# A fused attention and feed-forward kernel: small products in one 64x64 form, states by 48-wide updates

## The chip, the cores and the metric

The kernel runs on one core of a Trainium2 chip. A core has TensorE (PE in the profile; its weight loads are PEld), VectorE (DVE), ScalarE (ACT), GpSimd (POOL), SyncE (SP, which issues the loads and stores here) and 16 DMA engines. TensorE reads SBUF and writes PSUM, eight banks of 2 KB for each of 128 partitions. The metric is device time in microseconds of one launch.

## The reference

Inputs are fp32 or float64; batch 4, 8 heads, 768 tokens, head size 48, model width 384.

```python
for t in range(S):                                   # attention, per batch and head
    cur = np.einsum('bhd,bhe->bhde', u[None] * kt, vt)
    y[:, :, t] = np.einsum('bhd,bhde->bhe', rt, state + cur)
    state = wt[:, :, :, None] * state + np.einsum('bhd,bhe->bhde', kt, vt)
...
h = gelu(x @ w_in)                                   # x = y, heads side by side
u, v = h[..., :512], h[..., 512:]
v_n = (v - mean(v)) / sqrt(var(v) + 1e-6) * g_ln
v_s = einsum('ts,bsd->btd', w_sg, v_n) + b_sg        # over the 768 tokens
x = x + (u * v_s) @ w_out
...
gate = sigmoid(causal convolution of x over 5 tokens)
out = (gate * (x @ w_val)) @ w_out2
```

## The kernel before

**Attention** is worked in chunks of C = 64 tokens. A unit is one batch, one segment of 256 tokens (four chunks, NC) and one pair of heads (head 0 on partitions 0 to 63, of which 48 hold data, head 1 on 64 to 127); `unit(n)` holds its steps and there are 48 of them, 12 to a batch. The words in the order list are the steps' letters with a number. F and E: scans along the tokens for the decay factors (`suffix`, `prefix`). L and K: r and k times these factors. t and s: `turn`, two 128x128 transposes of k, and `scores`, eight 64x64 products of k and r into one PSUM bank, which m masks. B: `kv`, k by v for each chunk, and in batches 0 and 1 (`SUMMED = 2`) two products of r*k (q) with `u_col` for the r*u*k sums. o (`own_v`): the sums times v into y. d, a, S, p and D: `kv_out` copies kv's product into a strided tile, `states` runs a scan of 288 elements over it, `s_part` and `keep` copy the states out, `chunk_decay` spreads the decays. C: `tokens`, for each chunk the states and the masked scores by v. y: `y_out` adds to y on VectorE.

Both heads share a product in `kv` and `tokens`: the contraction runs over 128 rows, the right side is 96 wide and holds zeros where a head does not belong (tiles SE, `sv` and `vcd`; `pack_v` writes the zeros of `sv` on the host, `v_rows`, word v, copies into `vcd`). These are 128x64 forms: 128 rows, 64 columns of the array. In batches 2 and 3 `bonus` makes the r*u*k sums from loads of r and k by token (rk): a product on GpSimd, one on VectorE with `u_bc`, a VectorE reduction, a GpSimd product with v.

**The rest** works on half batches of 384 tokens. Each fp32 operand is split into two fp32r parts, and three 128x128 matmuls make one product (`PASS`). `xT` transposes y; `hv` makes v (512 wide) and layer norm in `ln`; `u_step` makes u; `vs_step` multiplies v_n by w_sg and scales (vso); `gated` forms u times that (gate); `wo_step`, `conv`, `val_step` and `out_step` follow. Accumulators of xT, hv, u, vs and val come from the PSUM pool psD (tag d, three buffers), those of wo and out from psC (c0 to c2), those of attention from psA (a0 and a1, one bank each) and in batch 0 also from psC and psD.

Weights arrive as float64 bits and are turned into fp32 by five passes on ScalarE and VectorE (`to_f32`, word dec) and split (`split`, spl: a copy on ScalarE, a remainder on GpSimd). In batch 0 `warm` puts three and two bf16 matmuls of 256 columns ahead of each `kv` and `tokens`; 16 of 512 columns (wps) stand at the start.

Batch b+1's attention is interleaved with batch b's rest; batch 0's attention stands alone at the start, beside the weights. All calls are recorded under words (`u13`, `vs7`, `C20`; at most `SIZE` calls to a word) and then issued in the order of `SCHEDULE`, a list written out in the source of some 2,600 words. Each engine works its own calls in that order; SP's loads have their places in the same list (pk, sv, rk, nat, wl, sg).

Of the kernel before, what the change touches and what calls it, by code (L numbers as in the profile page):

```python
# [15 lines left out]
F32 = mybir.dt.float32  # L16
# [7 lines left out]
DM = H * D  # L24
# [20 lines left out]
SV = 2 * NC * D  # L45
# [6 lines left out]
SIZE = dict.fromkeys(("hv", "u", "vs", "wo", "val", "out", "ln"), 3)  # L52
SIZE.update(dict.fromkeys("FvS", 2), z=2)

SCHEDULE = """
pk0 z0 zp4 pk1 ld0 ld1 nat0 pk2 zp0 pk3 wl0 wps0 zp7 zp5 zp1 zp3 a0 zp8 zp11 zp2 F0 wl2 D0 K0 E0 wl1
nat1 zp9 pk4 zp6 F1 L0 sv3 q0 K1 a3 E1 sv0 t0 t1 F2 k0 L1 pk5 v0 s0 a1 q1 K2 B0 v1 m0 E2 sg2 zp12 D1
zp13 k1 F3 L2 t2 o0 d0 s1 k2 sv1 a0 o0 B1 E3 D2 dec0 sv6 q2 L3 s2 o1 m1 v3 dec0 sg1 K3 d1 m2 dec1
dec0 o1 t3 wl3 dec2 dec1 pk6 v2 B2 a1 pk7 dec0 dec1 pk8 q3 o2 F4 d2 sv2 o2 D3 k3 sg0 a2 dec2 K4 s3
E4 B3 zp10 S1 F5 L4 S0 dec2 C1 K5 m3 v4 a2 t4 sv13 wl4 pk9 d3 sv7 k4 dec1 dec2 sv9 q4 B4 E5 sv5 dec0  # L60
t5 pk11 s4 k5 dec2 sv8 D4 C0 p0 a3 o4 pk10 d4 o4 spl0 y1 dec1 o3 S2 C2 o3 F6 p2 spl0 D5 nat2 S3 y0
sv4 C3 a4 v5 sv10 L5 spl1 y2 D6 E6 spl4 p1 spl2 q5 L6 y3 xT0 spl5 F7 s5 K6 S4 B5 m4 xTo0 E7 spl1 v6
m5 xTo0 xT1 F8 t6 hv0 K7 k6 d5 hv0 xTo1 q6 dec3 K8 xTo1 B6 a5 E8 D7 hv1 spl3 q7 L8 o6 d6 F9 s6 spl2
hv1 m6 q8 t7 t8 hv1 L7 k8 a6 dec4 hv0 o5 dec4 ln0 dec3 D8 dec4 k7 E9 p3 s7 ln1 F10 L9 S5 q9 v8 B8
spl3 ln0 S6 sg3 dec3 wl5 ln0 p6 v7 dec3 B7 o6 dec3 o5 ln0 C6 spl9 K9 m7 o7 d7 p4 a7 ln0 s8 spl9 p5
C5 ln1 dec4 o7 t9 E10 k9 d8 K10 nat3 pk12 v10 dec4 D9 spl5 v9 B9 y5 wl8 ld2 wl6 a8 spl4 F11 s9 d9
v11 C4 ln0 sg4 sg5 pk13 y6 S7 C7 y4 a9 K11 D10 dec5 m8 q12 t10 ln1 m9 E11 t11 k11 ln1 o8 S8 dec5 o8
q10 L10 p7 o9 y7 xT2 k10 F12 spl7 B10 o9 spl10 q13 D11 L11 dec5 xT3 s10 xTo3 K12 E12 S9 q11 B11 L12
d10 m10 xTo2 dec5 spl10 pk14 wl7 sv11 xTo2 hv2 xTo3 hv2 dec5 spl7 s12 F13 spl11 wl9 s11 ln1 spl11
t12 dec6 hv2 m11 dec6 C8 ln1 dec7 m12 d11 E13 hv3 k12 spl6 hv3 o10 v12 dec7 C9 a10 K13 S10 q14 t13  # L70
dec7 hv3 D12 dec6 spl8 dec7 o11 dec6 ln2 o11 y9 C10 a11 L13 ln2 S11 C11 spl8 ln3 dec6 o10 B12 a13
y11 dec7 ln2 nat4 sv12 pk15 y10 spl13 F14 D13 spl13 d12 o12 v13 y8 a12 ln2 xT4 xT5 spl12 E14 s13 ln2
spl12 a12 dec9 xTo4 L14 xTo4 hv4 S12 K14 ln2 ln3 hv4 xTo5 pk16 dec8 hv4 k13 dec8 spl6 xTo5 hv5 F15
u0 o12 u0 dec9 ln3 hv5 dec8 ln3 C12 dec9 dec8 B13 dec9 dec8 u0 dec9 spl14 wl12 hv5 E15 o13 wl10 D14
sv14 wl13 spl14 wl11 ln3 m13 a14 F16 ln5 s14 ln4 L15 vs0 y12 u1 q15 ln3 ln4 t14 vs0*2 a15 K15 ln4
dec10 u1 uo0 dec10 pk17 dec10 spl15 dec10 vs1 ln4 d13 dec10 K16 ln4 u1 a13 vs1 k14 ln4 cw0 ln5 D15
vs1 uo1 vs0 E16 ln5 dec12 vs1 dec11 m14 vs2 dec12 S13 vs2 ln5 dec11 vs0 ln5 dec12 dec11 s15 F17 ln5
vs2 dec12 vs2 ix1 dec13 C13 v14 dec13 vs0 o13 dec11 vs2*2 i0 dec13 dec11 B14 dec12 dec13 spl17 vs1
d14 dec13 spl17 spl16 vs1 vso2 wl15 sv15 wl14 wl16 t15 vso0 vs3 k15 spl16 gate0 vs3 m15 vs3 gate0
spl15 vso1 o14 vs3 a14 vs3 ix2 dec15 t16 gate0 vs3 v15 dec15 u2 o14 S14 y13 u2 dec15 L16 u2 gate1  # L80
dec14 dec15 p14 s16 p12 spl18 dec14 E17 C14 p13 spl18 gate1 B15 gate1 dec14 dec16 K17 u3 o15 dec14
d15 o15 uo2 wo0 dec16 D16 wo1 q16 wo4 dec14 q17 u3 spl19 dec16 u3 dec15 spl19 vso3 wo2 uo3 m16 wo5
k16 gate2 L17 sg6 sv16 u5 y14 gate2 dec16 wo3 pk19 pk18 u4 gate3 u5 a15 gate3 u5 spl20 dec16 S15 t17
gate3 spl20 s17 gate2 v16 C15 ix0 spl21 sg7 B16 sv17 wo8 spl21 d16 y15 uo5 q18 u4 spl22 u4 sg8 k17
F18 spl22 spl23 wo6 D17 wo9 E18 v17 xT6 spl23 sg9 wo7 uo4 woo0 xTo6 wo10 F19 spl24 vs4 woo0 sg10
spl24 vs4 x20 woo0 o16 wo11 woo1 cv0 L18 vs4 sg11 nat5 woo2 woo1 B17 a16 spl25 woo2 spl25 woo1 spl26
u6 m17 S16 cv0 u6 spl26 xTo6 u6 spl27 cv0 x22 vs4 spl27 v18 vs4 cv0 vs4 woo2 o16 x21 K18 xT7 cv1
# [12 lines left out]
x23 t24 woo4 ln7 hv9 x24 a23 cv3 hv8 woo4 o23 k24 o23 y22 S23 wo23 cv3 hv8 K26 cv4 bon0 v24 C23 cv4  # L100
woo5 hv8 y23 x25 cv4 woo5 hv9 m24 D25 bon0 ln8 hv9 F27 val3 ln9 bon0 val3 ln7 ln8 rk1 sv24 xT10 ln7
B24 xTo10 cv4 s25 v25 xTo10 t25 ln8 cv3 d24 hv10 L26 woo5 hv10 bon0 cv4 cv5 hv10 m25 cv4 a24 val3
ln10 E27 val4 k25 cv5 S24 xT11 valo3 B25 xTo11 C24 cv3 valo3 cv5 D26 s26 sv26 L27 outo1 nat7 valo3
val4 bon1 xTo11 t26 cv3 val4 ln8 cv3 u8 bon1 val5 valo4 val5 bon1 valo4 val5 cv5 ln8 rk2 pk28 u8
valo4 ln8 out9 cv5 hv11 a25 ln10 cv5 bon1 k26 out11 ln9 hv11 ln10 bon2 out10 valo5 u8 y24 ln9 F28
out12 uo8 hv11 ln9 u9 ln10 ln9 K27 u9 bon2 ln11 pk29 ln9 out14 d25 ln10 vs8 valo5 u9 ln10 valo5 vs8
uo9 ln11 out15 u10 m26 vs8 ln11 bon2 vs8 ln11 rk3 sv25 E28 u10 ln11 a25 s27 ln11 u10 S25 out13 v26
ix6 vs8*2 bon2 B26 vso8 C25 gate8 u11 K28 L28 gate8 D27 u11 gate8 uo10 ix7 t27 d26 vs9 outo3 k27
bon3 vs9 outo3 vs10*2 bon3 i2 u11 bon3 y25 vs9 rk4 pk30 a26*2 out16 F29 vs10 D28 outo4 out17 m27
wo24 outo5 vs10 S26 wo25 bon4 v27 vs9*2 bon4 vs9 K29 B27 vso9 C26 v28 a27 bon4 gate9 s28 rk5 sv27  # L110
nat8 p25 sv28 d27 vs10 p24 a27 p26 uo11 vs10 gate9 vs11 vso10 vs11 E29 vs11 gate10 L29 vs11 gate9
# [12 lines left out]
pk36 uo15 K35 vs15 S33 m34 E35 vs14 wo36 y32 L35 xTo14 vs15 bon8 ix10 pk37 outo7 outo8 wo39 k34 vs15
# [883 lines left out]
```

## Time and profile before

| | us |
|---|---|
| median of 3 runs (lowest, highest) | 526.92 (525.73, 529.72) |
| the profiled execution | 525.27 |
| its span, first to last instruction | 523.5 |
| PE busy | 494.8 |
| DVE busy | 414.2 |
| ACT busy | 301.2 |
| POOL busy | 197.9 |

Busy shares count the time in which an engine has an instruction under way. Matmuls are pipelined: a record of TensorE lasts from its start to its modelled end, some 0.2 us longer than the slot it takes, so the pace is read from starts. The granted clock is the share of 2.4 GHz that TensorE got. Nearly all instructions are recorded by one helper and have one line (930), so groups are told apart by their tiles. Rooms (room_l, room_w and the like) are places in tiles of later stages that attention uses in batch 0.

### The profile page before, as it was taken

The page shows a single profiled execution, that of the slowest core. Times are in us where ns is not written, and L with a number is a line of the kernel's source. Part 1 is how long each engine was busy: PE and PEld are TensorE (multiplying, and loading weights), DVE is VectorE, ACT ScalarE, POOL GpSimd, SP SyncE. Part 2 cuts the span into 40 slices and gives each one's busy share as a digit, 9 for nine tenths or more (in the row PEclk, how much of TensorE's full clock was granted, in tenths as well). Part 3 has the DMA queues.
Part 4 walks back from the last instruction along what each step waited for, and adds up shares of the span by engine and source line. Part 5 has one row for each costly group of instructions (what it writes and reads, how often), then busy time and mean ns, then how long its engine had stood idle before and what let it go on. Part 6 is the DMA issues. An engine that isn't in the chain of part 4 may idle for free. (4 is left out here: it accounts for less than half of the span.)

```text
span 523.5 us, 10670 instructions
## 1 busy us (share of the span) xinstructions
PE 494.8 (95%) x4060; PEld 435.5 (83%) x4060; DVE 414.2 (79%) x879; ACT 301.2 (58%) x719; POOL 197.9 (38%) x226
## 2 busy tenths in 40 slices
PE   7797878999999999999999999999999999999996
PEld 4564656798989897899888888899989988999995
DVE  7968878999899599966899689975986589624983
ACT  3677576556776657554575667543774665322443
POOL 6454756756732224572322241563004013600200
PEclk9679699899999999999999999999999999999999
DMA  8880352423523623424306342035123110000002
GB/s 301 321 268 9 127 165 81 138 103 106 166 77 92 175 84 90 140 77 159 114 2 207 105 149 73 17 122 170 42 92 92 35 43 1 16 31 0 1 2 91
DMA packets 27076, 53.44 MB, mean 102 GB/s; under 512 B 3088, under 2 KB 17168, under 8 KB 27024
## 3 DMA queue, kind: packets, MB, share of 16 engines
q1 hardware_dynamic: 27024, 52.75, 31.3%
q8 instruction: 32, 0.52, 0.4%
q14 instruction: 20, 0.16, 0.1%
HBM read 48.02 MB, written 4.72 MB: 101 GB/s over the span
## 5 line engine op out<-in xcount | busy, mean ns | idle before, releaser
L930 PE MATMUL vps<-wsg,vnt 128*128 128x384 f32 x576 | 119.2, 341 | 2.1 <-DVE gt L930 0.7
L930 PEld LDWEIGHTS vps<-wsg,vnt 128*128 128x128 f32 x576 | 100.0, 188 | 4.7 <-DVE gt L930 1.0
L930 POOL TENSOR_TENSOR L<-pk,E 128x256 f32<-128x256 f32 x38 | 30.3, 797 | 103.7 <-DVE E L930 41.4
L930 PE MATMUL hv<-win,x 128*128 128x512 f32 x216 | 62.0, 417 | 1.9 <-ACT x L930 1.4
L930 PE MATMUL ups<-x,win 128*128 128x384 f32 x288 | 62.9, 342 | 0.4 <-DVE gl L930 0.4
L930 PE MATMUL c<-gl,late 128*128 128x384 f32 x288 | 60.6, 339 | 0.0
L930 PEld LDWEIGHTS ups<-x,win 128*128 128x128 f32 x288 | 50.9, 188 | 1.5 <-DVE gl L930 0.5
L930 PEld LDWEIGHTS c<-gl,late 128*128 128x128 f32 x288 | 50.3, 188 | 1.5 <-DVE gl L930 0.4
L930 ACT ACTIVATE SE<-SD 64x192 f32<-64x192 f32 x80 | 45.0, 562 | 10.5 <-DVE SD L930 9.8
L930 DVE SCALAR_TENSOR_TENSOR cvp<-x,cw_col,cvp 128x384 f32<-128x384 f32 x84 | 49.8, 613 | 0.4
L930 PEld LDWEIGHTS hv<-win,x 128*128 128x128 f32 x216 | 40.1, 195 | 10.4 <-DVE x L930 2.0
L930 PE MATMUL o<-late,ml 128*128 128x384 f32 x216 | 47.9, 343 | 0.4 <-ACT ml L930 0.2
L930 POOL TENSOR_TENSOR vnt<-vg,vnt 128x512 fp32r<-128x512 f32 x24 | 33.8, 1415 | 33.4 <-ACT vnt L930 33.4
L930 PE MATMUL val<-x2hl,late 128*128 128x384 f32 x216 | 45.8, 344 | 0.0
L930 POOL TENSOR_TENSOR x<-x 128x384 f32<-128x384 f32 x24 | 27.1, 1135 | 48.9 <-DVE cvp L930 44.5
L930 DVE TENSOR_TENSOR_SCAN SD<-SD,SD 128x288 f32<-128x288 f32 x48 | 38.1, 795 | 8.0 <-ACT SD L930 7.6
L930 PEld LDWEIGHTS o<-late,ml 128*128 128x128 f32 x216 | 37.6, 188 | 3.3 <-DVE ml L930 1.3
L930 PEld LDWEIGHTS val<-x2hl,late 128*128 128x128 f32 x216 | 37.2, 188 | 1.9 <-DVE ml L930 0.5
L930 DVE SCALAR_TENSOR_TENSOR vps<-vps,misc,b_bc 128x384 f32<-128x384 f32 x29 | 17.9, 619 | 22.4 <-PE vps L930 22.4
L930 ACT ACTIVATE gl<-vps 128x384 fp32r<-128x384 f32 x29 | 14.2, 489 | 36.9 <-DVE vps L930 31.8
L930 DVE TENSOR_TENSOR_SCAN F<-pk,D1F 128x260 f32<-128x260 f32 x40 | 30.7, 767 | 3.3 <-DMA pk<-in_pk_dram 3.0
L930 ACT ACTIVATE vcd<-v 64x192 f32<-64x192 f32 x84 | 30.1, 358 | 5.0 <-PE bc L930 2.6
(162 smaller groups left out, 1026.3 us busy)
## 6 DMA issues: line engine op xcount, KB each, us to landing
pk<-in_pk_dram SPq DMA_DIRECT2D x40, 386.5 KB, 3.6
sv<-in_sv_dram SPq DMA_DIRECT2D x39, 192.0 KB, 3.1
v<-in_v_dram SPq DMA_DIRECT2D x12, 384.0 KB, 4.1
out_dram<-ot SPq DMA_DIRECT2D x24, 192.0 KB, 2.0
rk<-in_rk_dram SPq DMA_DIRECT2D x12, 384.0 KB, 3.1
bits<-in_w_in_dram SPq DMA_DIRECT2D x6, 512.0 KB, 6.2
room_l<-in_pk_dram SPq DMA_DIRECT2D x7, 386.5 KB, 7.4
bits<-in_w_o_dram SPq DMA_DIRECT2D x7, 384.0 KB, 4.7
```

Source lines behind the costliest of these rows:

```text
L930: f(*a, **k)
```

## The change

- `tokens` and `kv` multiply each head and chunk alone, in 64x64 tiles of the array with a right side of 48; four tiles take turns (`TILES`). The two row halves write two PSUM banks. The zeros in `sv`, SE and `vcd` go, and with them the steps v and S; `sv` loads are half as large. `scores` writes the same half that it reads.
- The r*u*k sums are products of 64x64 tiles with one column of `u_col`, eight to a unit, in all batches. `bonus`, the rk loads and `u_bc` go; q and o run in every unit.
- States: `grown` (g) copies kv's product of three chunks out of PSUM with the chunk's decay as scale, `states` (a) adds the decayed state before it (two or three 48-wide `scalar_tensor_tensor`), `carry` (z) and `carried` (U) hand the last one to the next segment. The scan of 288 and the steps D, d, S, p go.
- Layer norm: the centring goes to ScalarE with its sign turned (mean minus v), the scale goes into the split's copy, and the remainder is one VectorE `scalar_tensor_tensor`. The signs are turned back in vso and in the residual (`RES`). Remainders of the weight splits in `put_weights` go from GpSimd to VectorE.
- PSUM: psA holds a0 and a pair of banks p, psD has two buffers, batch 0's odd units take psC.
- Warm-up: six and four matmuls ahead of `kv` and `tokens` in batch 0, and 60 more in its first five steps.
- `SCHEDULE` is another list of some 2,700 words, with the words g, U, z, ox, yx and wm.

```diff
-SV = 2 * NC * D
+SV = NC * D
...
-    psD = ctx.enter_context(tc.tile_pool(name="psD", bufs=3, space=bass.MemoryType.PSUM))
+    psD = ctx.enter_context(tc.tile_pool(name="psD", bufs=2, space=bass.MemoryType.PSUM))
...
-    WB, WC = 3, 2
+    WB, WC = 6, 4
...
-            split(to_f32(bits, plain, t), dst[:, 0], dst[:, 1])
+            split(to_f32(bits, plain, t), dst[:, 0], dst[:, 1], dve)
...
-                    pe.matmul(out=sc[half[1 - hh], c, :], lhsT=kh[half[hh], c * C:(c + 1) * C],
+                    pe.matmul(out=sc[half[hh], c, :], lhsT=kh[half[hh], c * C:(c + 1) * C],
                               rhs=L[half[hh], 0, c * C:(c + 1) * C], start=True, stop=True)
...
         def kv():
-            t["b"] = shared(n)[:, 2 * NT * D:] if not first else ps(1, n, [128, 512])
-            warm(t["b"], WB)
+            o = t["b"] = shared(n)
+            warm(o[0], WB)
             for j in range(NT):
-                for hh in range(2):
-                    pe.matmul(out=t["b"][half[hh], 2 * j * D:(2 * j + 2) * D],
-                              lhsT=kn[:, j * 128 + 64 * hh:j * 128 + 64 * hh + 64],
-                              rhs=vcd[:, j, :, hh * D:(hh + 1) * D], start=True, stop=True)
-            if summed:
-                for j in range(NT):
-                    pe.matmul(out=t["b"][:, NC * D + 2 * j:NC * D + 2 * j + 2],
-                              lhsT=q[:, j * 128:(j + 1) * 128], rhs=u_col[:, 2 * p:2 * p + 2], start=True, stop=True)
+                for c2, hh in TILES:
+                    pe.matmul(out=o[c2][half[hh], j * D:(j + 1) * D],
+                              lhsT=kn[half[c2], j * 128 + 64 * hh:j * 128 + 64 * hh + 64],
+                              rhs=vt[b, s][half[c2], j, (2 * p + hh) * D:(2 * p + hh + 1) * D],
+                              start=True, stop=True)
+            for j in range(NT):
+                    for hh, c2 in TILES:
+                        c = 2 * j + c2
+                        pe.matmul(out=o[hh][half[c2], RS + j:RS + j + 1], lhsT=q[half[hh], c * C:(c + 1) * C],
+                                  rhs=u_col[half[hh], 2 * p + hh:2 * p + hh + 1], start=True, stop=True)
...
+        def grown():
+            for c in range(NC - 1):
+                with step("gx"):
+                    act.activation(out=st[:, c + 1], in_=t["b"][c % 2][:, c // 2 * D:(c // 2 + 1) * D],
+                                   func=AF.Copy, scale=f3[:, c + 1, 0:1])
+
+        def carried():
+            if s:
+                act.activation(out=st[:, 0], in_=cy, func=AF.Copy, scale=f3[:, 0, 0:1])
 
         def states():
-            if s == 0:
-                dve.memset(d1[:, :, 1], 0.0)
-            dve.tensor_tensor_scan(out=SD1, data0=SD1, data1=SD0, initial=0.0,
-                                   op0=ALU.add, op1=ALU.mult)
...
+            for c in range(0 if s else 1, NC - 1):
+                dve.scalar_tensor_tensor(out=st[:, c + 1], in0=st[:, c], scalar=f3[:, c + 1, 0:1],
+                                         in1=st[:, c + 1], op0=ALU.mult, op1=ALU.add)
+
+        def carry():
             if s < NSEG - 1:
-                act.activation(out=d1[:, :, 1], in_=d1[:, :, NC + 1], func=AF.Copy)
+                dve.tensor_tensor(out=cy, in0=t["b"][1][:, D:2 * D], in1=st[:, NC - 1], op=ALU.add)
 
         def tokens():
-            t["c"] = shared(n + 1)[:, 0:2 * NT * D] if not first else ps(2, n, [128, 512])
-            warm(t["c"], WC)
-            t3 = t["c"][:, 0:NT * 2 * D].rearrange("p (j e) -> p j e", j=NT)
-            for c in range(NC):
-                o = t3[half[c % 2], c // 2, :]
-                for i, rhs in enumerate((S, sv)):
-                    pe.matmul(out=o, lhsT=L[:, i, c * C:(c + 1) * C], rhs=rhs[:, c], start=(i == 0),
-                              stop=(i == 1))
+            o = t["c"] = shared(n + 1)
+            warm(o[0], WC)
+            for j in range(NT):
+                for i in range(2):
+                    for hh, c2 in TILES:
+                        c = 2 * j + c2
+                        none = s == 0 and c == 0
+                        if none and i == 0:
+                            continue
+                        pe.matmul(out=o[hh][half[c2], YC + j * D:YC + (j + 1) * D],
+                                  lhsT=L[half[hh], i, c * C:(c + 1) * C],
+                                  rhs=(sv if i else st)[half[hh], c],
+                                  start=(i == 0 or none), stop=(i == 1))
...
+    TILES = (0, 1), (1, 0), (0, 0), (1, 1)
...
     def shared(n):
         if n not in both:
-            both[n] = psA.tile([128, 512], F32, tag="a1", name="bc")
+            if n < NSEG * NP and n % 2:
+                both[n] = [psC.tile([128, 512], F32, tag=f"c{1 + i}", name=f"p{i}") for i in range(2)]
+            else:
+                a = psA.tile([128, 2, 512], F32, tag="p", name="p")
+                both[n] = [a[:, 0], a[:, 1], a]
...
-            dve.tensor_scalar(out=vg, in0=vg, scalar1=mv[:, 0:1], scalar2=rs, op0=ALU.subtract,
-                              op1=ALU.mult)
+            act.activation(out=vg, in_=vg, func=AF.Identity, scale=-1.0, bias=mv[:, 0:1])
             hi = vnt[b][:, 0, i, :]
-            act.activation(out=hi, in_=vg, func=AF.Copy)
-            pool.tensor_tensor(out=vnt[b][:, 1, i, :], in0=vg, in1=hi.bitcast(F32), op=ALU.subtract)
+            act.activation(out=hi, in_=vg, func=AF.Copy, scale=rs)
+            dve.scalar_tensor_tensor(out=vnt[b][:, 1, i, :], in0=vg, scalar=rs, in1=hi.bitcast(F32),
+                                     op0=ALU.mult, op1=ALU.subtract)
...
+        if n < 5:
+            for _ in range(4):
+                with step("wm"):
+                    for _ in range(3):
+                        pe.matmul(out=wps[:, 256:512], lhsT=wsrc[:, 0:128], rhs=wsrc[:, 0:256], start=True, stop=True)
```

## Rows read from the trace of the kernel before

**Rows 1.** The page: busy time, share and instructions of each engine; granted TensorE clock by slices.
```profile
PE 494.8 (95%) x4060; PEld 435.5 (83%) x4060; DVE 414.2 (79%) x879; ACT 301.2 (58%) x719; POOL 197.9 (38%) x226
...
PEclk9679699899999999999999999999999999999999
```

**Rows 2.** Stretches: length, busy time (instructions) of PE, PEld, DVE, ACT, POOL; clock, DMA share, GB/s.
```profile
10.00:20.00 10.00, 6.61 (x70) 4.90 (x69) 9.84 (x22) 5.33 (x16) 5.12 (x9) 0.80 1.04 382
20.00:30.00 10.00, 9.31 (x71) 6.78 (x72) 8.54 (x15) 4.36 (x11) 3.13 (x5) 0.50 0.66 221
...
50.00:60.00 10.00, 9.17 (x81) 6.87 (x82) 8.17 (x16) 6.52 (x18) 7.83 (x10) 0.50 0.30 93
...
100.00:500.00 400.00, 393.71 (x3210) 360.34 (x3209) 316.88 (x681) 227.75 (x540) 137.01 (x147) 1.00 0.28 86
```

**Rows 3.** Timeline of PE, a unit of batch 1: start, busy, engine, line, operation, count.
```profile
157.31 0.34 PE L930 MATMUL bc<-sv,L 128*64 128x96 f32 x4
157.48 0.39 PE L930 MATMUL bc<-SE,L 128*64 128x96 f32 x4
157.65 0.39 PE L930 MATMUL bc<-sv,L 128*64 128x96 f32 x4
157.81 0.55 PE L930 MATMUL bc<-vcd,kn 128*64 128x96 f32 x8
158.29 0.61 PE L930 MATMUL bc<-misc,rk 128*128 128x2 f32 x4
158.76 0.78 PE L930 MATMUL o<-late,ml 128*128 128x384 f32 x3
159.37 0.38 PE L930 MATMUL a<-ident,kh 128*128 128x128 f32 x2
```

**Rows 4.** Timeline of PE, a later unit, and the large matmuls behind it.
```profile
348.42 0.39 PE L930 MATMUL bc<-sv,L 128*64 128x96 f32 x4
348.74 0.68 PE L930 MATMUL a<-L,kh 64*64 64x64 f32 x16
349.35 0.79 PE L930 MATMUL o<-late,ml 128*128 128x384 f32 x3
349.98 0.69 PE L930 MATMUL ups<-x,win 128*128 128x384 f32 x3
350.51 0.51 PE L930 MATMUL vps<-wsg,vnt 128*128 128x384 f32 x2
```

**Rows 5.** Groups on PE: shapes, count, busy us, mean ns of one, idle before.
```profile
L930 PE MATMUL a<-D1F 128*128 128x256 bf16 x60 | 13.1, 326 | 0.0
```

**Rows 6.** Groups on DVE.
```profile
L930 DVE TENSOR_TENSOR_SCAN SD<-SD,SD 128x288 f32<-128x288 f32 x48 | 38.1, 795 | 8.0 <-ACT SD L930 7.6
...
L930 DVE SCALAR_TENSOR_TENSOR vps<-vps,misc,b_bc 128x384 f32<-128x384 f32 x29 | 17.9, 619 | 22.4 <-PE vps L930 22.4
L930 DVE TENSOR_SCALAR vg<-vg,mv,rstd 128x512 f32<-128x512 f32 x24 | 16.6, 697 | 2.8 <-POOL rstd L930 2.6
...
L930 DVE TENSOR_TENSOR gl<-vps,gl 128x384 fp32r<-128x384 f32 x29 | 15.9, 547 | 6.8 <-ACT gl L930 6.8
...
L930 DVE TENSOR_TENSOR y<-bc,y 128x192 f32<-128x192 f32 x36 | 12.5, 347 | 9.0 <-ACT SD L930 5.2 <-PE bc L930 3.7
...
L930 DVE TENSOR_TENSOR rk<-pk 128x256 f32<-128x256 f32 x12 | 5.3, 438 | 1.4 <-DMA pk<-in_pk_dram 1.4
...
L930 DVE TENSOR_SCALAR rstd<-mv 128x1 f32<-128x1 f32 x24 | 3.7, 154 | 0.8
```

**Rows 7.** Groups on ACT.
```profile
L930 ACT ACTIVATE SE<-SD 64x192 f32<-64x192 f32 x80 | 45.0, 562 | 10.5 <-DVE SD L930 9.8
...
L930 ACT ACTIVATE gl<-vps 128x384 fp32r<-128x384 f32 x29 | 14.2, 489 | 36.9 <-DVE vps L930 31.8 <-PE c L930 3.1 <-PE o L930 1.2
...
L930 ACT ACTIVATE SD<-SD 128x48 f32<-128x48 f32 x32 | 8.9, 293 | 0.3
...
L930 ACT ACTIVATE rsw<-bc 128x4 f32<-128x4 f32 x12 | 2.0, 169 | 0.5 <-PE bc L930 0.4
```

**Rows 8.** Groups on POOL.
```profile
L930 POOL TENSOR_TENSOR vnt<-vg,vnt 128x512 fp32r<-128x512 f32 x24 | 33.8, 1415 | 33.4 <-ACT vnt L930 33.4
```

More of the change, by code (lines that the diff above doesn't have):

```diff
@@ L59 @@
[L59 to L63, printed above, removed]
@@ L450, in causal @@
                               in1=mask.unsqueeze(1).to_broadcast([128, NC, C]))
-        def v_rows():
-            for c2 in range(2):
-                act.activation(out=vcd[half[c2], :, c2, :],
-                               in_=vt[b, s][half[c2], :, 2 * p * D:(2 * p + 2) * D], func=AF.Copy)
         def warm(o, k):
-            for _ in range(k if first else 0):
-                pe.matmul(out=o[:, 256:512], lhsT=wsrc[:, 0:128], rhs=wsrc[:, 0:256], start=True, stop=True)
+            if first:
+                with step("wm"):
+                    for _ in range(k):
+                        pe.matmul(out=o[:, 256:512], lhsT=wsrc[:, 0:128], rhs=wsrc[:, 0:256], start=True, stop=True)
@@ L477, in own_v @@
+            for x, i in pair(t["b"]):
+                with step("ox"):
+                    act.activation(out=rs[:, i], in_=x[:, :, RS:RS + NT], func=AF.Copy)
             if p == 0:
@@ L494, in s_part @@
-        def s_part():
-            for hh in range(2):
-                act.activation(out=S[half[hh], :, hh, :], func=AF.Copy,
-                               in_=d1[half[hh], :, 1:NC + 1].rearrange("p e c -> p c e"))
-        def keep():
+                               in1=rs.rearrange("p h j -> p j h").unsqueeze(3).to_broadcast([128, NT, 2, D]))
+        def grown():
[3 more added lines that the diff above has]
+                                   func=AF.Copy, scale=f3[:, c + 1, 0:1])
@@ new lines, in y_out @@
+        def y_out():
+            for x, i in pair(t["c"]):
+                hd = lambda a: a.rearrange("p j (h e) -> p j h e", e=D)[:, :, i]
+                y = hd(yt[b, s][:, :, 2 * p * D:(2 * p + 2) * D])
+                z = x[:, :, YC:YC + NT * D].rearrange("p h (j e) -> p j h e", e=D)
+                with step("yx"):
+                    dve.tensor_tensor(out=y, in0=z, in1=y, op=ALU.add)
+        steps = {"F": suffix, "E": prefix, "L": r_part, "K": k_part, "q": ruk,
+                "t": turn, "s": scores, "k": k_rows, "m": causal,
+                "B": kv, "o": own_v, "g": grown, "U": carried, "a": states, "z": carry,
@@ L535, in ps @@
-    def ps(i, n, shape):
-        if i == 2 and n % 2 == 0:
-            return psD.tile(shape, F32, tag="d", name="a2")
-        if units[n][0] == 0 and n % 2:
-            return psC.tile(shape, F32, tag=f"c{i}", name=f"a{i}")
-        return psA.tile(shape, F32, tag=f"a{i}", name=f"a{i}")
-    loads = {"pk": load_unit, "sv": load_sv, "rk": load_rk}
-    loaded, user = {"pk": 0, "sv": 0, "rk": SUMMED * KS}, {}
+            if n < NSEG * NP and n % 2:
[3 more added lines that the diff above has]
+                both[n] = [a[:, 0], a[:, 1], a]
@@ L546, in run_loads, with pair, bank @@
+        return both[n]
+    def pair(o):
+        if len(o) == 3:
+            return [(o[2], slice(0, 2))]
+        return [(x.unsqueeze(1), slice(i, i + 1)) for i, x in enumerate(o)]
+    def bank(n):
+        ring, tag = (psC, "c0") if units[n][0] == 0 and n % 2 else (psA, "a0")
+        return ring.tile([128, 512], F32, tag=tag, name="a0")
+    loads = {"pk": load_unit, "sv": load_sv}
+    loaded, user = {"pk": 0, "sv": 0}, {}
     def run_loads(kind, done, most=NU):
-        while loaded[kind] < (B * KS if kind == "rk" else NU) and most > 0:
+        while loaded[kind] < NU and most > 0:
```

366 lines of the change are left out of this document (163 added, 203 removed).

## The prediction

> **What bounds the kernel now.** I read the page's busy shares and clock slices first, then the table by stretches, then the timeline of TensorE. TensorE is busy 95% of the span, VectorE 79%, and TensorE's clock is below full speed in the first fifth only [rows 1]. The table by stretches splits the run. From 100 to 500 us TensorE is busy 393.7 of 400 us at granted clock 1.00 (2.4 GHz), VectorE 316.9; before that TensorE has gaps, and stretches at 0.50 (1.2 GHz) [rows 2]. A busy TensorE could still hide waits, so look at the timeline: three matmuls of 384 columns start 0.53 us before the next three, with nothing between [rows 4]. So from 100 us on TensorE's order sets the time, and a microsecond taken from it is a microsecond gained; before 100 us loads, VectorE and the cold clock share the limit.
>
> There are 48 attention units (batch, segment, head pair), 12 to a batch. Batch 0's fall before about 100 us; the other 36 are interleaved with the large matmuls of the stretch that TensorE bounds. In the trace each fp32 product is two matmul records.
>
> **Small products, per unit.** Before, tokens() gives 16 records of 96 columns in the 128x64 form: groups of four start 0.167 us apart on average, 0.67 us a unit. kv() gives 8: 0.48 us from its start to the start of the next form, of which two groups of four are 0.33 and the change of form is 0.15 [rows 3]. scores() gives 16 records of 64 columns in the 64x64 form: 0.61 us, 0.46 without the 0.15 of leaving [rows 4]. Sum 0.67 + 0.33 + 0.46 = 1.46 us, changes of form apart.
>
> After, tokens() gives 32 records of 48 columns, kv() 16, the r*u*k sums 16 of one column, and scores() its 16. What does a record cost when four 64x64 tiles take turns? No row shows four tiles at work. Two rows bound it. A record of the sums before streams 2 columns but loads 128 weight columns, and four take 0.47 us, 0.117 each [rows 3]: the load sets that pace, and 64 columns at the same pace are 0.058. Scores run 16 records in two tiles in 0.46 us, so a tile starts one every 0.058 us, and two tiles run side by side [rows 4]. The 128x64 form shows the other direction: records of the two column halves overlap, since four in 0.167 us is a pair in 0.083, while each streams 96 columns [rows 3]. So I take four tiles side by side, each at 0.058 us a record: 64 records / 4 x 0.058 = 0.93 us, plus 0.46 for scores (still two tiles) = 1.39 us. That is 0.07 less a unit, 36 x 0.07 = **2.5 us gained**. Halving the columns gains almost nothing, since the weight load, not the columns, sets the pace. The lower bound is columns alone, 48/96 of 0.083 = 0.042 per tile and record: 0.67 + 0.46 = 1.13 us, 11.9 us gained in all. The upper bound is two tiles at a time, 0.029 us a record as scores now: 64 x 0.029 + 0.46 = 2.32 us, 36 x 0.86 = 31 us lost.
>
> A page speaks against the change here: the Trainium skill, "TensorE: Matmul & The Clock Gate", section "Wait — 56ns, not 53.3ns?", gives a floor of about 25 ns from one matmul's start to the next, however few the columns. By it the 64 records would take 1.6 us and the case below that is slow would stand near 536; scores at 29 ns a record don't contradict it, and no row here is faster over a whole product.
>
> **The sums before.** Batches 0 and 1 form them by four records of 0.117: 0.47 us a unit [rows 3]. Their new cost is in the 1.39. Batch 1's 12 units give back 12 x 0.47 = **5.6 us**. Batches 2 and 3 formed them on GpSimd and VectorE (bonus()), off TensorE; that is removed.
>
> **Changes of form.** A run of tokens, kv and scores before changes from 128x128 to 128x64 to 64x64 and back, and the old sums went through 128x128 as well. Reading TensorE's words in both SCHEDULE lists, units 12 to 47 have 121 changes before and 85 after. One costs 0.15 us: four token records that end a form take 0.32 us against 0.167, and the first three large matmuls behind a form take 0.63 against 0.53 [rows 4]. 36 x 0.15 = **5.4 us gained** (0.10 to 0.20: 3.6 to 7.2).
>
> **States, copies, layer norm, loads: costed at nothing on the path.** VectorE loses the scan of 288 (48 x 0.795 = 38.1 us), the normalisation (16.6) and bonus()'s two passes. It gets 128 updates and 32 carries of 48 columns (0.15 to 0.35 us each, the cost of 1 and of 192 columns as bounds; I take 0.25: 40 us), 24 more r*k products (0.44: 10.6 us), 24 scalar_tensor_tensor on 512 columns (0.619 x 512/384 = 0.82: 19.8 us) and 16 splits of weights at 0.55 to 0.75 (9.6 us) [rows 6]. In and out are about 75 us each, so VectorE stays near 415 us; from 100 to 500 us it has 83 us to spare [rows 2], which is the cover. If that cover were gone TensorE would wait for L, kn or a PSUM drain. ScalarE loses the SE copies (45.0 us) and the strided copies around them, and gets 144 + 32 copies of 48 columns (0.17 to 0.35; below 0.293 as they are contiguous), and 24 passes of 512: a net loss of work on an engine at 58% [rows 1, 7]. GpSimd loses 33.8 us of layer norm remainders, the bonus products and the weight splits, and gets 24 products for own_v [rows 8]. SP's queue has 12 rk loads fewer and half the sv bytes; nothing waits longer for that.
>
> **PSUM.** psD goes from three buffers to two, since the small products now take two banks per unit. A vps tile is held behind its last matmul for 0.62 + 0.56 + 0.49 + 0.55 = 2.2 us (vso, product with ut, split on ScalarE, remainder) [rows 6, 7], the product priced as the remainder. With two buffers the second-next tile waits for that, unless wo, out or attention words stand between. SCHEDULE after puts such words there; summing TensorE's costs between a tile's last word and the tile that reuses its buffer, I find about as much uncovered time as before, 0 to 10 us more if each drain starts 1 us late. I take **2 us lost**.
>
> **The first 100 us.** Weight splits (10 of the 16 fall here, 6 us) and 32 updates with 8 carries (10 us) come to VectorE, 12 scans (9.5 us) leave: about 6 us more for it. ScalarE is freed, 12 sv loads are halved. There are 120 more warm-up matmuls of 256 columns; before, 60 of them held 13.1 us [rows 5]. In 10 to 20 us TensorE was busy 6.6 of 10 and the clock fell to 0.50 in the next stretch, where TensorE is busy 9.3 of 10, so limiting; likewise 50 to 60 us [rows 2]. If the fillers hold the clock at 1.00 those two stretches could each be some 4 us shorter, of which VectorE, busy 8.5 and 8.2 of 10, allows about 1.5 each. I take **3 us gained**; 8 gained to 8 lost.
>
> **Sum.** The profiled execution took 525.3 us (span 523.5 and 1.8 around it): 525.3 - 2.5 - 5.6 - 5.4 + 2 - 3 = 510.8. The median of the runs shown, 526.9, is 1.6 above it: 512.4, so **512 us**.
>
> **Rivals.**
> - **Two tiles at a time** (slower). If starts or loads of the small records share one pace, the 64 records cost 0.029 each: 31 us lost in place of 2.5 gained, 512 + 34 = 546. For it: no row is faster than 0.029 over a product. Against it: neighbours in different tiles overlap in both directions. It decides from 0.021 us a record, where 36 x (64 x 0.021 - 1.00) = 12.4 us eats the other terms (12.0 gained).
> - **The gain becomes waits.** Two psD buffers, and VectorE at 415 of 512 us, stop TensorE at drains: 10 us for psD, and a microsecond more for some units; 521 to 529. For it: the 2.2 us of a vps tile. Against: stretches of the present order are covered.
> - **A longer start.** The fillers stand in TensorE's order ahead of products that others wait for, and VectorE has 6 us more: 8 lost in place of 3 gained, 523.
> - **The change does not do what it says:** the 48-column products take as long as 96-column ones per tile (0.083 a record). Then 1.33 + 0.46 = 1.79 us a unit, 12 us lost in place of 2.5 gained, 527; I count it with the waits.
>
> **Chances.** Four tiles, as summed: 0.57, own range 500 to 521. Two tiles or one pace: 0.22. Waits, with the last rival: 0.14. Longer start: 0.07. About 1% (5.2 us) is what a measurement here can tell from no change: faster is below 521.7, slower above 532.2. Faster: 0.55 of the first case, 0.03 of the waits, 0.03 of the longer start: 0.61. Slower: the 0.22 and 0.01 of the waits: 0.23. Within 1%: the rest, 0.16. Range: from 500 (loads cheaper than columns, all of the start's gain: 498) to 540, which takes in waits, the longer start and a pace between 0.021 and 0.026; beyond it lie about 0.16 of the two-tile case and 0.03 below.
>
> **What would show it.** 32 token records of 48 columns from first to last in about 0.47 us (four tiles) or 0.93 (two); the r*u*k sums in about 0.23; no 128x64 form; 5940 matmuls or slightly fewer; the granted clock near 1.00 in 20 to 30 and 50 to 60 us; TensorE's idle time from 100 us on, put down to DVE gl or vps, below 10 us. A visit of tokens, kv, sums and scores beyond 2 us proves the sum wrong at its first term; large matmuls more than 0.18 us apart with attention unchanged prove it wrong at psD.

## The result, and the profile after

The changed kernel takes 508.21 us (median of 4, 506.32 to 509.97) against 526.33 us for the kernel before (525.67 to 529.72): a ratio of 0.9643, 95% interval 0.9581 to 0.9704. Measured again beside the last experiments it stands at 504.98 (504.77 to 506.16) against 526.02, 0.9612 (0.9582 to 0.9643). The forecast was 512 with a range of 500 to 540: the gain came, and 4 to 7 us more of it. The first profiled execution took 509.97 us, that of the repeat 504.83; both are used below.

The page of the changed kernel, to be read beside [rows 1]: busy time, share and instructions of each engine, and the granted clock by slices.

```profile
PE 480.2 (94%) x5940; PEld 427.6 (84%) x5940; DVE 409.5 (81%) x997; ACT 233.1 (46%) x629; POOL 124.5 (24%) x173
...
PEclk9796999899999999999999999999999999999999
```

TensorE has 5940 matmuls in place of 4060 and is busy 14.6 us less. The busy time of VectorE, ScalarE and GpSimd has not grown; VectorE's share of the shorter span has (79% before, 81% now). The stretches of [rows 2] (length, busy time of PE, PEld, DVE, ACT, POOL, then clock, DMA share, GB/s):

```profile
10.00:20.00 10.00, 6.54 (x125) 5.17 (x126) 7.01 (x17) 2.90 (x8) 2.93 (x5) 0.79 1.04 404
20.00:30.00 10.00, 8.19 (x102) 6.03 (x100) 8.86 (x24) 3.51 (x11) 3.86 (x4) 0.87 0.55 198
...
50.00:60.00 10.00, 9.25 (x118) 6.54 (x118) 6.95 (x21) 4.45 (x13) 2.94 (x5) 0.83 0.05 17
...
100.00:500.00 400.00, 394.89 (x4625) 365.68 (x4624) 326.35 (x790) 189.45 (x501) 88.12 (x120) 1.00 0.23 68
```

From 100 us on the picture is that of before: TensorE busy 98.7%, clock 1.00. Now the timeline of TensorE over one visit of tokens, kv and sums, against [rows 3] (start, length, engine, operation, count):

```profile
408.74 0.33 PE L917 MATMUL p<-st,L 64*64 64x48 f32 x8
408.89 0.30 PE L917 MATMUL p<-sv,L 64*64 64x48 f32 x8
409.00 0.30 PE L917 MATMUL p<-st,L 64*64 64x48 f32 x8
409.12 0.30 PE L917 MATMUL p<-sv,L 64*64 64x48 f32 x8
409.24 0.41 PE L917 MATMUL p<-v,kn 64*64 64x48 f32 x16
409.47 0.37 PE L917 MATMUL p<-misc,q 64*64 64x1 f32 x16
409.77 0.50 PE L917 MATMUL hv<-win,x 128*128 128x512 f32 x1
```

The 32 token records hold 0.50 us (408.74 to 409.24), where [rows 3] had 16 in 0.67; kv's 16 hold 0.23, and the 16 of the sums 0.30 with the change of form behind them. Another visit has scores between tokens and kv. Its unit is the first segment of a batch, whose first chunk has no state before it, so its tokens have 28 records:

```profile
314.83 0.34 PE L917 MATMUL val<-x2hl,late 128*128 128x384 f32 x1
315.10 0.26 PE L917 MATMUL p<-st,L 64*64 64x48 f32 x2
...
315.53 0.23 PE L917 MATMUL a<-L,kh 64*64 64x64 f32 x1
315.54 0.22 PE L917 MATMUL p<-sv,L 64*64 64x48 f32 x2
315.60 0.47 PE L917 MATMUL a<-L,kh 64*64 64x64 f32 x10
315.86 0.26 PE L917 MATMUL p<-v,kn 64*64 64x48 f32 x2
315.89 0.28 PE L917 MATMUL a<-L,kh 64*64 64x64 f32 x3
...
316.12 0.18 PE L917 MATMUL p<-misc,q 64*64 64x1 f32 x1
...
316.27 0.39 PE L917 MATMUL p<-misc,q 64*64 64x1 f32 x9
316.59 0.61 PE L917 MATMUL o<-late,ml 128*128 128x384 f32 x2
```

Tokens run from 315.10 to where scores take over at 315.53 to 315.60: 28 records in 0.43 to 0.50 us. All four products with their 76 records are through in 1.49 us, the change of form behind them included. And kv's first records (315.86) start between scores that are still running.

Where the time went, by TensorE's records: the run is cut at the first vps matmul, behind which nearly the same work is left in all three (1,574 or 1,568 matmuls of 384 columns, 69 or 71% of the small records). From there each record is charged with the time to the next start. Large matmuls and transposes count at a floor (0.175 us for 384 columns, 0.233 for 512, 0.109 for 128), and what lies above it is waits and changes of form. Stops of TensorE among the small products are counted in that row too.

| us | before | changed, 509.97 | changed, 504.83 |
|---|---|---|---|
| up to the first vps matmul | 104.3 | 108.7 | 102.6 |
| from there: small products and sums | 68.5 | 52.1 | 51.8 |
| large matmuls and transposes at their floor | 326.5 | 325.0 | 325.0 |
| what lies above the floors, and waits | 19.8 | 18.0 | 19.4 |
| from there, in all | 414.8 | 395.1 | 396.2 |

So the gain is made behind the start: 19 us there, of which the small products give 16.5. The 1.5 us in the row of floors are not saved: six matmuls of 384 columns and four transposes stand ahead of the cut in the changed kernel. What two executions of the changed kernel differ by lies ahead of it. In the start the small products' slots fell as well, from 42.0 to 27.5 us, and the fillers' (at 0.109 each) rose from 8.3 to 21.4.

### The profile page after: what moved, and what is told of

It reads as the page before. It is cut to its first block, busy times and chain, and to the rows that moved or that the text cites. A ratio compares the mean times of both kernels' runs of the same rounds, so it can differ in the third digit from the quotient of the medians.

```text
span 508.2 us, 14436 instructions
## 1 busy us (share of the span) xinstructions
PE 480.2 (94%) x5940; PEld 427.6 (84%) x5940; DVE 409.5 (81%) x997; ACT 233.1 (46%) x629; POOL 124.5 (24%) x173
## 4 chain that ended last, share of the span: by engine, by line
PE 62%; DVE 19%; ACT 3%; issue 3%; DMA 1%; POOL 1%; ACTq 0%; DVEq 0%; POOLq 0%; SPq 0%
PE vps L917 16%; PE ups L917 7%; PE p L917 7%; PE c L917 7%; PE o L917 7%; PE val L917 7%; PE hv L917 6%; PE a L917 5%; DVE st L917 2%; DVE spare L917 2%; DVE F L917 2%; DVE E L917 1%; DVE cvp L917 1%; DVE vps L917 1%; DVE gl L917 1%
## 5 line engine op out<-in xcount | busy, mean ns | idle before, releaser
L917 PE MATMUL vps<-wsg,vnt 128*128 128x384 f32 x576 | 114.3, 341 | 1.3 <-DVE gl L917 1.2
L917 POOL TENSOR_TENSOR L<-pk,E 128x256 f32<-128x256 f32 x38 | 28.2, 742 | 137.2 <-PE p L917 54.2
L917 PE MATMUL ups<-x,win 128*128 128x384 f32 x288 | 60.8, 343 | 0.1
L917 ACT ACTIVATE st<-p,F 128x48 f32<-128x48 f32 x144 | 38.0, 301 | 43.9 <-PE p L917 42.5
L917 DVE SCALAR_TENSOR_TENSOR st<-st,F 128x48 f32<-128x48 f32 x128 | 39.2, 307 | 15.7 <-ACT st L917 14.3
L917 POOL TENSOR_TENSOR y<-v,rsw 128x192 f32<-128x192 f32 x48 | 26.1, 546 | 82.6 <-ACT rsw L917 81.4
L917 PE MATMUL val<-x2hl,late 128*128 128x384 f32 x216 | 43.0, 340 | 0.2 <-DVE ml L917 0.2
L917 ACT ACTIVATE gl<-vps 128x384 fp32r<-128x384 f32 x29 | 14.2, 491 | 49.2 <-DVE vps L917 39.2
L917 POOL TENSOR_TENSOR x<-x 128x384 f32<-128x384 f32 x24 | 25.2, 1062 | 47.1 <-DVE cvp L917 47.1
L917 DVE TENSOR_TENSOR_SCAN F<-pk,D1F 128x260 f32<-128x260 f32 x40 | 29.6, 740 | 3.6 <-DMA pk<-in_pk_dram 3.3
L917 PEld LDWEIGHTS <-D1F 128*128 128x128 bf16 x196 | 19.6, 108 | 13.0 <-issue 7.2
```

Source lines behind the costliest of these rows:

```text
L917: f(*a, **k)
```

## Experiments

The kernel before stood at 524.95 to 526.51 us in these comparisons; a ratio is always to it on the same chip. "The changed kernel" is 505 where no other number is given.

**Two tiles at a time, and one.** kv(), the sums and tokens() with the tile outside:

```diff
-            for j in range(NT):
-                for c2, hh in TILES:
+            for j, G in [(j, G) for G in GROUPS for j in range(NT)]:
+                for c2, hh in G:
```

GROUPS is TILES[0:2], TILES[2:4] in the first run and four single tiles in the second.

> The same products in another order: within kv(), the r*u*k sums and tokens(), all products of the two tiles (0,1) and (1,0) come first, then all of (0,0) and (1,1). Theory A (the gain is that four tiles run at once, each at 0.058 us a record, and a tile's products must stand near each other in program order for it): two tiles at a time, 32 turns of 0.058 in place of 16, 0.93 us more a unit, 36 x 0.93 = 33 us in the stretch that TensorE bounds: about 541 us; a little less where the end of one pair overlaps the start of the next. Rival B (each tile has a queue of its own that looks far enough ahead, or the pace doesn't hang on which tiles alternate): 506 to 511 us, the 58 ns between records of one tile unchanged.

> The same products again, now tile by tile: kv() gives all four products of one tile, then the next tile's, and so do the sums and tokens(). Theory A (tiles run side by side only when neighbours in program order are in different tiles): 64 records one after another at 0.058 are 3.7 us a unit against 0.93, 36 x 2.8 = 100 us more: about 608 us. Rival B (a queue per tile, deep enough for eight records): 506 to 515 us. If e1_pairs is slower by about 33 us and this by about 100, the weight load of one tile can't overlap its own matmuls and order is what the gain rests on.

Measured: 511.64 us in pairs (0.9735, 0.9684 to 0.9785), 533.00 tile by tile (1.014, 1.0084 to 1.0196). Neither theory holds: the runs are 7 and 28 us longer, a fifth and a quarter of what a strict order would cost. The timeline of TensorE in the second shows why; from 313.69 on it is tokens alone:

```profile
313.53 0.23 PE L918 MATMUL a<-L,kh 64*64 64x64 f32 x2
313.58 0.22 PE L918 MATMUL p<-sv,L 64*64 64x48 f32 x1
...
313.69 0.32 PE L918 MATMUL p<-st,L 64*64 64x48 f32 x4
313.81 0.32 PE L918 MATMUL p<-sv,L 64*64 64x48 f32 x4
313.97 0.32 PE L918 MATMUL p<-st,L 64*64 64x48 f32 x4
314.08 0.32 PE L918 MATMUL p<-sv,L 64*64 64x48 f32 x4
314.24 0.32 PE L918 MATMUL p<-st,L 64*64 64x48 f32 x4
...
314.84 0.44 PE L918 MATMUL c<-gl,late 128*128 128x384 f32 x1
```

A tile has eight records here, and a new tile comes in every 0.275 us (313.69, 313.97, 314.24). In the single starts, read by the program's order of st and sv, one tile's records stand 0.058 us apart, and the next tile's first record starts 6 ns after the fifth of the one before, ahead of three records that stand earlier in the program. So a few records that wait for their tile let later ones of another tile pass, more of them don't: two tiles overlap by about half. In the changed kernel's order, where neighbours are in different tiles, all four run. This supports the account of four tiles from the other side: the order matters, and the pace of one tile does not change.

**The diagonal first.**

```diff
-    TILES = (0, 1), (1, 0), (0, 0), (1, 1)
+    TILES = (0, 0), (1, 1), (0, 1), (1, 0)
```

> One line: the tiles are taken in the order (0,0), (1,1), (0,1), (1,0) in place of (0,1), (1,0), (0,0), (1,1). scores() writes its 64x64 products into the tiles (0,0) and (1,1) and stands just before kv() or after tokens(). Theory A (part of the gain that the sum did not count is that kv's first products, in tiles that scores does not use, run beside the last scores): up to two records of 0.058 less overlap at each of two joints a unit, 36 x 0.06 to 0.12 = 2 to 4 us more, 510 to 512 us. Rival B (each tile's products start as soon as that tile is free, whatever the order of neighbours): 508 us within 1, and kv's records of the other two tiles still start beside the scores.

Measured: 505.03 us (0.9611, 0.9564 to 0.9659), the same as the repeat of the changed kernel (0.9612). B holds: which tile comes first is worth nothing that can be measured.

**The sums in their old form.**

```diff
-                    for hh, c2 in TILES:
-                        c = 2 * j + c2
-                        pe.matmul(out=o[hh][half[c2], RS + j:RS + j + 1], lhsT=q[half[hh], c * C:(c + 1) * C],
...
+                    pe.matmul(out=o[0][:, RS + 2 * j:RS + 2 * j + 2], lhsT=q[:, j * 128:(j + 1) * 128],
+                              rhs=u_col[:, 2 * p:2 * p + 2], start=True, stop=True)
```

> The changed kernel with the r*u*k sums in the form of before, in all units: two products of 2 columns over 128 rows in place of eight of 1 column over 64; all else stays. Theory A (four records of 0.117 us, loads of 128 columns, and a change of form more a unit): 0.47 us in place of 16 records / 4 tiles x 0.058 = 0.23, and 36 more changes at 0.15: 36 x (0.24 + 0.15) = 14 us longer, 521; the order list's own changes from kv to what follows stay. Rival B (the sums' cost in the new form is not the load: 16 issues cost as much as four): under 5 us longer, 507 to 512.

Measured: 521.12 us (0.9900, 0.9859 to 0.9941), 16 us longer by the medians and 15 by the ratios, where A had 14. In the profile 10.5 of them lie behind the first vps matmul (406.7 us against 396.2) and the rest ahead of it, in the part that differs between executions too. The timeline of TensorE after the last kv record:

```profile
315.69 0.40 PE L916 MATMUL p<-v,kn 64*64 64x48 f32 x10
316.02 0.61 PE L916 MATMUL p<-misc,q 128*128 128x2 f32 x4
316.48 0.41 PE L916 MATMUL a<-ident,kh 128*128 128x128 f32 x2
```

Four sums hold 0.46 us again, as in [rows 3], though they stream 2 columns.

**Tokens in their old form.**

```diff
-                    for hh, c2 in TILES:
-                        pe.matmul(out=o[hh][half[c2], YC + j * D:YC + (j + 1) * D],
-                                  lhsT=L[half[hh], i, c * C:(c + 1) * C],
-                                  rhs=(sv if i else st)[half[hh], c],
+                        pe.matmul(out=o[j][half[c2], YC:YC + 2 * D],
+                                  lhsT=L[:, i, c * C:(c + 1) * C],
+                                  rhs=(sv if i else st)[:, 1 + j:3 + j],
```

> The changed kernel with tokens() in the form of before in its cost: eight products of 96 columns over 128 rows into 64 rows in place of sixteen of 48 over 64 (it sums both heads and takes neighbouring chunks, so attention's output is another; nothing else is changed, and the states' and loads' halved size stays). Theory A (my sum: 16 records at 0.167 us for four are 0.67 us in place of 0.47, and by the order list 48 more changes of form at 0.15): 36 x 0.2 + 48 x 0.15 = 14 us longer, 521. Rival B (the gain of the change lies elsewhere, in fewer waits for VectorE and GpSimd, and the form is worth nothing): within 3 us of 507. Rival C (only the change of form counts): 7 us longer, 514.

Measured: 518.88 us (0.9876, 0.9831 to 0.9921), 14 us longer, as A had it, 13 of them behind the first vps matmul (409.2 us). Its timeline of TensorE:

```profile
318.71 0.39 PE L914 MATMUL p<-st,L 128*64 128x96 f32 x4
318.93 0.34 PE L914 MATMUL p<-sv,L 128*64 128x96 f32 x4
319.09 0.39 PE L914 MATMUL p<-st,L 128*64 128x96 f32 x4
319.25 0.39 PE L914 MATMUL p<-sv,L 128*64 128x96 f32 x4
319.57 0.51 PE L914 MATMUL a<-L,kh 64*64 64x64 f32 x10
```

Tokens hold 0.86 us with the change to scores' form (0.32 for the last four records against 0.16), 0.36 more than above; 36 times that is 13. The two kernels together lose 23.5 us behind the first vps matmul, more than the whole change gained there: the mixed forms have more changes between them (110 and 122 in the records there, against 76 in the changed kernel and 116 before). So the two runs show that each product's form counts, but don't split the gain into parts, and kv's old form was not tried.

**Fewer fillers, and none.**

```diff
-    WB, WC = 6, 4
+    WB, WC = 0, 0
...
-        if n < 5:
+        if n < 0:
```

With the fillers of before, WB and WC are 3 and 2, and the 60 are left out as well.

> The changed kernel without any of the 180 warm-up matmuls inside batch 0 (the 16 at the very start stay). The first 104 us gained nothing: small products took 15.6 us less there and fillers 13.1 us more. Theory A (the fillers hold the clock up and are worth what they cost): without them the granted clock is at 0.50 in more of the first 100 us, products there take twice as long, and the run is 4 us or more longer: 511 to 520. Rival B (the fillers are what took the gain; TensorE's time in the start goes to them): 5 to 10 us shorter, 497 to 503. Rival C (loads and VectorE set the start, whichever clock TensorE has): within 2 us of 507.

> The changed kernel with the fillers of the kernel before: 3 and 2 a unit in place of 6 and 4, and none of the 60 after the first five units (120 fewer of 256 columns, some 13 us of TensorE's records). Theory A (fillers are worth what they cost): 2 us or more longer, 509 to 514, with more of the first 100 us at granted clock 0.50. Rival B (they took the gain): 3 to 8 us shorter, 499 to 504. Rival C (loads and VectorE set the start): within 2 us of 507. The three kernels with 180, 60 and 0 fillers together say on which side the optimum lies.

Measured: 506.00 us without (0.9628, 0.9582 to 0.9673), 505.90 with the old ones (0.9639, 0.9589 to 0.9688). Rival C holds. The stretches of the kernel without fillers:

```profile
20.00:30.00 10.00, 3.94 (x80) 3.53 (x80) 9.61 (x24) 3.01 (x8) 3.57 (x3) 0.50 0.51 181
30.00:40.00 10.00, 5.46 (x116) 4.39 (x116) 9.83 (x25) 5.37 (x19) 2.76 (x4) 0.50 0.81 236
...
0.00:100.00 100.00, 72.19 (x1144) 55.31 (x1145) 85.19 (x216) 43.72 (x128) 38.81 (x55) 0.69 0.48 164
```

and of the changed kernel's repeat:

```profile
20.00:30.00 10.00, 8.13 (x131) 6.31 (x132) 9.93 (x23) 4.14 (x11) 3.59 (x3) 1.00 0.48 179
30.00:40.00 10.00, 7.17 (x150) 5.41 (x145) 9.29 (x24) 5.25 (x17) 3.35 (x5) 1.00 0.90 256
...
0.00:100.00 100.00, 83.41 (x1389) 61.37 (x1390) 87.90 (x219) 45.49 (x131) 38.69 (x57) 0.93 0.51 171
100.00:500.00 400.00, 393.43 (x4553) 364.59 (x4551) 321.85 (x779) 187.81 (x499) 85.03 (x118) 1.00 0.21 66
```

Between 20 and 40 us the clock is at 1.2 GHz in the one and at 2.4 in the other, and the time is the same. Without fillers TensorE is idle for 4.5 to 6.1 of 10 us there, VectorE for 0.4 at most. It is VectorE that is full in these stretches.

**VectorE's work in the start.** State updates of batch 0 left out, and, in another run, r*k of batch 0 on GpSimd:

```diff
-            for c in range(0 if s else 1, NC - 1):
+            for c in range(0 if s else 1, NC - 1) if b else ():
```

```diff
-            dve.tensor_tensor(out=q, in0=r, in1=k, op=ALU.mult)
+            (pool if b == 0 else dve).tensor_tensor(out=q, in0=r, in1=k, op=ALU.mult)
```

> The changed kernel with the 32 state updates of 48 columns left out in batch 0 alone (its states are then not carried, so batch 0's output is another); in the stretch that TensorE bounds nothing is touched. They hold VectorE for 32 x 0.329 = 10.5 us of the first 104 us. Theory A (VectorE sets the length of the start, which is why neither fewer products nor fewer fillers nor a colder clock moved it): 5 to 10 us shorter, 497 to 502. Rival B (loads, or the chain through each unit, set it): within 2 us of 507. A shorter time by the chain alone, without VectorE's being full, would show as idle time of VectorE in the first 100 us above the 18 us that it has now.

> One word: in batch 0 the products r*k are made by GpSimd in place of VectorE (12 of 0.47 to 0.54 us, 6 us of VectorE's first 100; GpSimd pays 12 of some 0.8 us and is busy 36 of 100 there). Theory A (VectorE sets the start): 3 to 6 us shorter, 501 to 504. Rival B (VectorE is not the limit): within 2 us of 507. Rival C (GpSimd's products come late for kv and its sums): 2 us or more longer.

> The changed kernel itself once more, as the mark for the runs beside it: 505 to 510 us, since the kernel before stands at 525 on these chips and the ratio was 0.964.

Measured on one chip: 504.98 us for the changed kernel, 496.84 without the updates (0.9445, 0.9404 to 0.9486), 503.56 with r*k on GpSimd (0.9580, 0.9554 to 0.9607). Taking 10.5 us of VectorE out gave 8.1, the first vps matmul moved from 102.6 to 96.7 us, and VectorE stayed busy 86.5 of the first 100 (87.9 with the updates): this supports theory A, though the updates also stand between kv and tokens, so a shorter chain may have a part in it. Moving 6 us to GpSimd gave 1.4, which by the intervals is not told from nothing (all four runs do lie below the four of the changed kernel), and the first vps matmul stayed (102.9): GpSimd takes 0.82 to 0.87 us for a product that VectorE makes in 0.47 to 0.54, and VectorE then waits longer, for y from GpSimd (1.9 us in the first 104, 0.9 before the move) and for scores (2.8, 1.0 before). It is the fastest kernel here with all the work in it, by a margin that the runs don't settle.

**More work for VectorE behind the start.** Every state update of batches 1 to 3 is made twice (`idle` is a place that nothing reads); in a second run the same 96 instructions stand behind r*k instead, with r and k as operands:

```diff
+                if b:
+                    dve.scalar_tensor_tensor(out=idle, in0=st[:, c], scalar=f3[:, c + 1, 0:1],
+                                             in1=st[:, c + 1], op0=ALU.mult, op1=ALU.add)
```

> The changed kernel with every state update of batches 1 to 3 made twice (once into a place that nothing reads): 96 more instructions on VectorE, 96 x 0.307 = 29 us, VectorE at 439 us. Theory A (from 104 us on TensorE's order sets the time, VectorE's work is covered, and costing states, layer norm and bonus() at nothing was right): under 3 us longer, 507 to 510. Rival B (VectorE at 81% is at the edge; part of the change's gain or loss passed through it): 8 us or more longer, 515 to 536.

> The same 96 idle updates of 48 columns in batches 1 to 3 as in the run that made each state update twice (it stood at 533, 28 us above the changed kernel), but behind r*k, which is made a unit ahead, and not between kv and tokens. Theory A (place: idle work costs only where a unit's products wait for it, from kv over the updates to tokens): under 8 us longer than the changed kernel at 505, 505 to 513. Rival B (VectorE's whole order stands tight against TensorE's, through the two psD buffers and the single p: wherever 0.6 to 0.9 us is put in front, the next drain is late): 20 to 30 us longer, 525 to 535.

Measured: 533.30 us (1.0119, 1.0065 to 1.0173) and 528.38 (1.0039, 1.0008 to 1.0071): 28 and 23 us longer for 29 us of work. B holds in both. The group of the second, and then the five largest of its waits of TensorE from 104 us on (total, times, longest):

```profile
L921 DVE SCALAR_TENSOR_TENSOR idle<-pk,F 128x48 f32<-128x48 f32 x96 | 29.4, 307 | 2.1
```

```profile
PE vps L921 <- DVE gl L921: 5.5, 4, 3.8
PE p L921 <- DVE cy L921: 4.4, 5, 1.7
PE a L921 <- DVE x L921: 1.4, 2, 0.9
PE a L921 <- POOL L L921: 1.3, 2, 0.8
PE c L921 <- DVE gl L921: 1.2, 3, 0.8
```

All of TensorE's waits there come to 21 us; in the changed kernel's two profiles they are 3.6 and 5.2 (5.3 before), the longest 1.2. VectorE was idle 78 us of the 400 from 100 us on, and yet most of the added time reached the end. A reading that fits, argued and not tried by itself: each engine works a fixed order, VectorE's idle time lies where it waits for TensorE and ScalarE, and TensorE can run ahead of it by two psD tiles and one p at most. psD's third buffer could not be given back to try it alone, since the changed kernel fills all eight PSUM banks; what it would absorb here stays open.

## Why the prediction was right, and where not

**Four tiles at 0.058 us a record: right, shown.** The first term stood on two rows, a load that sets the pace at 2 columns and two tiles side by side. 32 token records took 0.46 us from the first start to the last and 0.50 to the next product, where 0.47 was forecast for four tiles and 0.93 for two, and records of one column have the pace of those with 48. So the rival of two tiles falls. One record in 15 ns, with records of different tiles 6 to 7 ns apart in the single starts, decides the other rival as well: the rule of the Trainium skill, "TensorE: Matmul & The Clock Gate", section "Wait — 56ns, not 53.3ns?", that starts are never under about 25 ns apart, does not hold for records in different 64x64 tiles here. The kernel before showed that already: its scores' records start 7 ns and some 52 ns apart by turns (from 348.74 us on), of which the prediction took only the mean, 29 ns, when it wrote that they don't contradict the rule. What the Trainium skill says in "TensorEngine Tiling (Array Packing)", section "Key Properties", is that tiles load weights and multiply in parallel, and that a change of the form drains TensorE. The trace fits both (32 records in 0.46 us at 0.058 us a tile; 0.32 us for the last four records of a form against 0.16), though it does not show the drain as such.

**Small products, sums and forms together: 13.5 us forecast, 16.5 measured** from the first vps matmul on. Two terms were tried from the other side, there too: the old tokens cost 13 us for 14, the old sums 10.5 for 14. The changes of form behind the first vps matmul fell by 40 in the records (116 to 76), where the order lists had 36. What the sum did not have is the overlap of scores with kv: it charged scores 0.46 us by themselves, and the timeline shows kv's records from some 0.3 us after scores begin. Its share was not measured by itself.

**psD: 2 us lost in the forecast, about 1 us by the trace.** The excess of the 384-column matmuls over 0.175 us, where no small product follows, went from 12.0 to 13.8 us, near the forecast, but that is not psD alone. A missing buffer would hold up the first matmul of a psD tile: there the excess went from 0.95 to 1.85 us, in both mostly one wait of vps near 119 us. Products into c, which is in psC, have 2.2 us more, and those inside vps tiles 1.7 less. The list of waits has that one wait for a drain:

```profile
PE vps L917 <- DVE gl L917: 1.2, 1, 1.2
```

With all eight banks filled, the third buffer could not be tried alone, so psD's price stays an estimate. TensorE's stops among the small products fell by 1.3 to 2.6 us, which the sum did not have.

**States, copies, layer norm at nothing: right number, wrong cover.** VectorE's total is 409.5 us for "near 415", but by luck. The prediction's own items add up to 80 us in (40, 10.6, 19.8 and 9.6) and not 75, and what left held 71, which would give some 424. In the trace 84 us came in: the 48-wide updates took 0.307 us where 0.25 was taken (39.2 us for 128), the carries 0.196. The busy time still fell, by 5 us: some 11 us went from instructions that stand in both kernels and became shorter, and more of VectorE's instructions overlap. The sum had neither, and no run explains them. The copies on ScalarE took 0.301 and 0.336 us, not below 0.293. And the 83 us to spare were not a cover, as the two kernels with idle updates show: 29 us more cost 28 and 23 us. That the term cost nothing fits VectorE's unchanged total and a SCHEDULE written anew for the new work; which of them counts was not tried.

**The first 100 us: 3 us gained in the forecast; measured 4.4 lost and 1.7 gained, and the reason wrong.** The clock did rise (0.50 to 0.87 and 0.83, in the repeat 1.00 in both stretches). The step that failed is "so limiting" of [rows 2]: TensorE busy 9.3 of 10 at 1.2 GHz was taken for the limit, though VectorE was busy 8.5. In the changed kernel without fillers the clock stays at 1.2 GHz for 20 us on end and nothing is lost; the kernel before was not tried with another clock. That the 14.5 us which the products saved there came to nothing fits the same reason: up to the first vps matmul VectorE is busy 90.5 us where it had 86.5, and leaving out its updates shortened the start. Why two executions of one kernel differ by 6 us in the start is open.

**The sum.** Behind the start 19 us were gained, 1.5 of them by work moved ahead of the cut (forecast 11.5), in the start between 4 lost and 2 gained (forecast 3): 15 to 20 us in the two profiled executions, 18 and 21 by the medians, 14.5 in the forecast.

## What to carry to other kernels

- Price a small fp32 product in 64x64 tiles by 0.058 us a record and tile, not by its columns (1, 48 and 64 were measured), and write neighbours into different tiles: four products go through in the time of one.
- Idle time need not be a cover where several engines follow one fixed order: before work is costed at nothing, ask which buffer lets the engine run late. And a stretch where the clock is low is worth a faster clock only if no other engine is full there.

## What the runs showed of the hardware

- A 64x64 tile starts an fp32 record every 0.058 us at 1, 48 or 64 columns, and four tiles do so at once (32 records in 0.46 us).
- Tiles overtake each other: with eight records of one tile in a row, the next tile's first starts 6 ns after the fifth, before three that stand earlier in the program (533 us in that order against 505).
- The change between the 128x64 and 64x64 forms cost 0.16 us (0.32 against 0.16 for four records).
